# An attention and two-layer expert kernel: the upper weight words scaled on ScalarE, the first weight chunks issued by ScalarE, and four blocks of probabilities normalised in one VectorE operation

## The chip, the cores and the metric

The kernel runs on one core of a Trainium2 chip. The metric is the device time of one execution in microseconds; the median of several runs is given. One core has TensorE (matrix products, transposes), VectorE, ScalarE, GpSimd and SyncE, which in this kernel issues almost all transfers. In the profile they are called PE (its weight loads PEld), DVE, ACT, POOL and SP (its queue SPq).

## What is computed

Inputs of the two dense layers come as 64-bit floats and everything else as 32-bit floats. The reference, cut:

```python
k_all = np.concatenate([k_g, k_l], axis=2)            # 4 batches, 8 heads, 32 + 512 keys, 64 wide
out_g = softmax(scale * q_g @ k_all^T) @ v_all        # 32 global queries see everything
s_ll = where(abs(i - j) <= 32, scale * q_l @ k_l^T, -1e9)
a_l = softmax(concatenate([scale * q_l @ k_g^T, s_ll]))
out_l = a_l @ concatenate([v_g, v_l])                 # 512 local queries see a window and the global keys
x = concatenate([out_g, out_l])                       # as 2176 rows of 512
h = x @ w_in                                          # 512 x 2048
x = maximum(0.01 * h, h) @ w_out                      # 2048 x 512
expert = argmax(normalised x @ normalised emb^T / tau)
out[rows of e] = gate * (maximum(x[rows of e] @ w1[e], 0) @ w2[e])   # 8 experts, 1024 wide
```

`softmax` is the exponential of the scores less their maximum, divided by its sum plus 1e-9.

## The kernel before

The program has three stages that overlap: attention, the two dense layers, and the routed experts. TensorE's instructions stand in the order in which the program is written; the order on ScalarE, VectorE, GpSimd and SyncE is made by a scheduler, from the same program, priorities and its own table of durations. Each engine then runs its list strictly in order.

**Attention** goes by pairs of heads (16 pairs, n) and by groups of two chunks of 128 queries (32 groups, p, called S in the code). For a pair, `QK` transposes keys and queries; for a group, `S` makes eight products (L200), adds the mask and takes the maximum on VectorE (L211), takes four exponentials with their sums on ScalarE (L217), adds 1e-9 and takes the reciprocal on VectorE (L221, L222), and scales the four blocks of 224 probabilities by their reciprocals: two of the four on VectorE (L228) and two on ScalarE (L226). The blocks lie in four tiles `pr`, one for each head of two groups in turn. Later `TR` transposes the probabilities and `AV` multiplies them with the values. The work is dealt out in 68 slots, the first 21 of them alone (up to the first dense step), the rest between the steps of the dense layers.

**The weights of the dense layers** come in 32 chunks of 128 x 512, alternately from `w_in` and `w_out`, as 64-bit floats, and are made into a 32-bit float and then into a high and a low part of it. `conv_load` loads a chunk of 512 KB into one of two buffers `raw` (L343, issued by SyncE). `conv_round` reads it twice on ScalarE: L359 takes the absolute value of the upper words as 32-bit floats, L360 scales the lower words to three bits. `conv_bits` works on VectorE: a maximum with a tiny number (L368), a shift by three with a mask (L369), an operation that puts in sign and top bit from the raw upper words (L372), and the addition of the low bits (L375). `conv_split` copies the high part on ScalarE (L382) and subtracts on GpSimd (L383). One call of `conv` does split(i - 1), bits(i), round(i + 1), load(i + 2). In the first 21 slots `conv` is called in each even slot from the second on (10 times); then once a step, and more often as the dense steps ask for their chunks.

**Dense layers**: `L1` is one step of the first product (L675, 12 matmuls), the leaky ReLU with its split into two parts (L682 and L685 on ScalarE, L683 and L686 on VectorE), `L2` the second product (L697 to L699).

**The start**: keys, queries and values of the first three pairs are loaded, all by SyncE, each issue of its own (`load_qk`, `load_v`, L88 to L119), then the first two chunks of the weights.

Of the kernel before, what the change touches and what calls it, by code (L numbers as in the profile page):

```python
# [18 lines left out]
P = 128  # L19
BIG = 3.0e38  # L20
NEG = -8.0e9
TINY = 1.125 * 2.0 ** -15


@with_exitstack
def kernel(
# [55 lines left out]
    def load_qk(n):  # L82
        b, h0 = n // HP, 2 * (n % HP)
        kn = att.tile([P, NC, 2, D], F32, tag="kn", bufs=2, name="kn")
        qn = att.tile([P, NC, 2, D], F32, tag="qn", bufs=1, name="qn")
        def rows(dst, src):
            for h in range(2):
                nc.sync.dma_start(dst[:, :, h, :], src[b, h0 + h].rearrange("(c p) d -> p c d", p=P))  # L88

        rows(kn, k_l)  # L90
        if n % 2 == 0:
            gn = att.tile([2 * SG, 4 * D], F32, tag="gn", bufs=2, name="gn")
            for i, src in enumerate((k_g, q_g)):
                nc.sync.dma_start(
                    gn[i * SG:(i + 1) * SG].rearrange("s (h d) -> s h d", h=4),
                    src[b, h0:h0 + 4].rearrange("h s d -> s h d"),
                )
        else:
            gn = natural["gn"]
        rows(qn, q_l)  # L100
        natural["gn"] = gn
        natural[n] = qn, kn, gn[:, (n % 2) * 2 * D:(n % 2 + 1) * 2 * D]
# [32 lines left out]
    )  # L135
    nc.gpsimd.memset(mask[:, 0, 0:SG], NEG)
    nc.gpsimd.memset(mask[:, 2, WIN - SG:WIN], NEG)
    NPR = 4
    prs = [att.tile([P, 2, 256], F32, name=f"pr{i}") for i in range(NPR)]
    qz = att.tile([P, NC * P], F32, name="qz")  # L140
    gzs = [att.tile([P, 2, SG], F32, name=f"gz{i}") for i in range(2)]
    for t in gzs:
# [48 lines left out]
    def S(p):  # L191
# [4 lines left out]
        for i in range(2):  # L196
            c = c0 + i
            for h in range(2):
# [2 lines left out]
                    sps[h][:, i, :], qz[r, c * P:(c + 1) * P], kT[r, c, :], start=True, stop=True,  # L201
                    tile_position=(D * h, 0),
                )
        pr2 = [prs[(2 * p + h) % NPR] for h in range(2)]
        nm = att.tile([P, 4], F32, tag="nm", bufs=2, name="nm")
        sm = att.tile([P, 4], F32, tag="sm", bufs=2, name="sm")
        for h in range(2):
# [12 lines left out]
            )  # L220
        nc.vector.tensor_scalar(out=sm, in0=sm, scalar1=1e-9, scalar2=None, op0=ALU.add)  # L221
        nc.vector.reciprocal(out=sm, in_=sm)  # L222
        for j in range(4):
            pr = pr2[j // 2][:, j % 2, 0:WK]
            if j % 2:
                nc.scalar.activation(out=pr, in_=pr, func=AF.Copy, scale=sm[:, j:j + 1])  # L226
            else:
                nc.vector.tensor_scalar(out=pr, in0=pr, scalar1=sm[:, j:j + 1], scalar2=None, op0=ALU.mult)  # L228
        for h in range(2):
            units[2 * p + h] = pr2[h]  # L230

# [100 lines left out]
    def conv_load(i):  # L332
        f = i // 2
        if i % 2 == 0:
            src = w_in[:, f * P:(f + 1) * P].rearrange("(k p) f -> p k f", p=P)
            shape = [P, KM, P]
        else:
            src = w_out[f * P:(f + 1) * P, :].unsqueeze(1)
            shape = [P, 1, DM]
        if wide:  # L340
            t = att.tile([P, 2 * DM], I32, tag="raw", bufs=2, name="raw")
            t = t.rearrange("p (k n) -> p k n", k=shape[1])
            nc.sync.dma_start(t, src.bitcast(I32))  # L343
            raws[i] = t.rearrange("p k (n t) -> p k n t", t=2)
        else:
            t = att.tile([P, DM], F32, tag="raw", bufs=2, name="raw")
            t = t.rearrange("p (k n) -> p k n", k=shape[1])
            nc.sync.dma_start(t, src)
            raws[i] = t

    def conv_round(i):

        if wide and i in raws:
            pair = []
            for k in range(2):
                t = sb.tile([P, DM], I32, tag=("x2T", "x2")[k], bufs=2, name=f"t{k}")
                pair.append(t.rearrange("p (k n) -> p k n", k=raws[i].shape[1]))
            temps[i] = pair
            nc.scalar.activation(out=pair[0].bitcast(F32), in_=raws[i][:, :, :, 1].bitcast(F32), func=AF.Abs)  # L359
            nc.scalar.activation(out=pair[1], in_=raws[i][:, :, :, 0].bitcast(U32), func=AF.Copy, scale=2.0 ** -29)  # L360

    def conv_bits(i):
        if not wide or i not in raws:
            return
        raw = raws.pop(i)
        top = raw[:, :, :, 1]
        t, low = temps[i]
        nc.vector.tensor_scalar(out=t.bitcast(F32), in0=t.bitcast(F32), scalar1=TINY, scalar2=None, op0=ALU.max)  # L368
        nc.vector.tensor_scalar(  # L369
            out=t, in0=t, scalar1=3, scalar2=0x3FFFFFF8, op0=ALU.logical_shift_left, op1=ALU.bitwise_and  # L370
        )
        nc.vector.scalar_tensor_tensor(  # L372
            out=t, in0=top, scalar=-0x40000000, in1=t, op0=ALU.bitwise_and, op1=ALU.bitwise_or
        )
        nc.vector.tensor_tensor(out=t, in0=t, in1=low, op=ALU.add)  # L375
        temps[i] = t

# [562 lines left out]
        )  # L940


    QK(0, 0)
    QK(0, 1)
    for t in prs:
        nc.vector.memset(t[:, :, WK:256], 0.0)
    for ve, vb in zip(ves, vbs):
        nc.vector.memset(ve[32:64, NC], 0.0)
        nc.vector.memset(vb[96:P], 0.0)
        nc.vector.memset(vb[32:64, NC - 1], 0.0)  # L950
    load_v(0)
    load_qk(1)
    load_qk(2)
    load_v(1)
    for i in range(2):
        conv_load(i)
    conv_round(0)

    NU = 4 * NHP
# [75 lines left out]
    SLOT0 = 21  # L1035
    while slot < SLOT0:
        run(att_parts(slot))
        if slot >= 2 and slot % 2 < 1:
            conv()
        if slot == 2:  # L1040
            routing_constants()
# [7 lines left out]
    k = 0  # L1049
# [167 lines left out]
```

## Time and profile before

| | us |
|---|---|
| median of 3 runs | 940.39 (939.21 to 940.49) |
| the profiled execution | 938.37 |
| its span, first to last instruction | 936.7 |
| TensorE busy in the span | 869.3 (93%) |
| VectorE busy | 640.6 (68%) |
| ScalarE busy | 586.4 (63%) |
| GpSimd busy | 169.2 (18%) |

Busy time is the time in which an engine ran an instruction that computes. Shares of the whole span are averages over stages with different limits, so each stage has to be read for itself. The chain of work that ended last goes 69% through TensorE, 12% through VectorE, 7% through transfers. The TensorE clock is granted by the chip in two levels, and the profile shows the mean of a stretch as a share of the higher one; over the span it is 0.961.

### The profile page before, as it was taken

To read this page: it belongs to the slowest core of one execution; us is meant where nothing else is said; L and a number is where in the kernel's file an instruction comes from. 1 tells how busy PE (TensorE), PEld (TensorE's weight loads), DVE (VectorE), ACT (ScalarE), POOL (GpSimd) and SP (SyncE) were. 2 spreads that over 40 slices of the span, in tenths; PEclk is the share of its full clock that TensorE was granted. 3 is DMA by queue.
4 is the path that set the end of the run, shared out by engine and by line. 5 is a ranking of instruction groups with operands and counts; after the bars stand their busy time and mean duration, and the time that the engine had idled before them with its cause. 6 is when DMAs were issued, how large, how long until landed. Compare 5 with 4: busy or idle time off the path is not lost.

```text
span 936.7 us, 16036 instructions
## 1 busy us (share of the span) xinstructions
PE 869.3 (93%) x5578; PEld 731.6 (78%) x5578; DVE 640.6 (68%) x1623; ACT 586.4 (63%) x1270; POOL 169.2 (18%) x220
## 2 busy tenths in 40 slices
PE   6567798899999999999999999997899999999997
PEld 4445686688888888888888888985677888888885
DVE  5589889953564554463543435555989989999996
ACT  5688777754545645554533233364687888888885
POOL 2232423310100110010000000030233232231211
PEclk9777889999999999999999999997999999999999
DMA  5766455311022011110000000544315118829550
GB/s 126 196 167 156 137 145 154 109 42 29 23 65 47 20 51 39 26 39 11 1 23 1 23 1 24 180 158 112 24 57 195 53 46 300 300 62 385 199 202 26
DMA packets 104997, 92.70 MB, mean 99 GB/s; under 512 B 73735, under 2 KB 82055, under 8 KB 104914
## 3 DMA queue, kind: packets, MB, share of 16 engines
q1 hardware_dynamic: 100690, 80.87, 28.7%
q0 software_dynamic: 4224, 10.78, 4.1%
q8 instruction: 45, 0.74, 0.4%
q14 instruction: 38, 0.31, 0.1%
HBM read 140.03 MB, written 11.63 MB: 162 GB/s over the span
## 4 chain that ended last, share of the span: by engine, by line
PE 69%; DVE 12%; DMA 7%; issue 6%; ACT 4%; SPq 1%; POOL 0%; POOLq 0%; DVEq 0%; ACTq 0%
PE hps L675 19%; PE hp L901 9%; PE yp L929 8%; PE yp L697 7%; PE yp L699 6%; PE yp L698 6%; DMA raw<-in_moe_w_in_dram 3%; PE sp L200 2%; PE pp L236 2%; PE av L250 2%; DVE t L372 2%; DMA raw<-in_moe_w_out_dram 2%; PE tp L915 1%; DVE w2s L856 1%; DVE w1s L856 1%
## 5 line engine op out<-in xcount | busy, mean ns | idle before, releaser
L683 DVE SCALAR_TENSOR_TENSOR gf<-gf 128x256 f32<-128x256 f32 (+1 forms) x144 | 60.4, 427 | 125.0 <-ACT gf L682 124.8
L682 ACT COPY gf<-hps 128x256 f32<-128x256 f32 (+1 forms) x144 | 50.2, 360 | 151.5 <-PE hps L675 150.3
L901 PE MATMUL hp<-w1s,xgT 128*128 128x512 f32 x528 | 138.9, 413 | 0.0
L929 PE MATMUL yp<-w2s,ht 128*128 128x512 f32 x528 | 130.9, 396 | 1.0 <-DVEq L1181 1.0
L929 PEld LDWEIGHTS yp<-w2s,ht 128*128 128x128 f32 x528 | 98.8, 188 | 25.7 <-DVEq L1181 1.4
L901 PEld LDWEIGHTS hp<-w1s,xgT 128*128 128x128 f32 x528 | 99.8, 196 | 21.3
L697 PE MATMUL yp<-woh,g 128*128 128x512 f32 x272 | 114.9, 423 | 0.2 <-ACT g L685 0.2
L699 PE MATMUL yp<-woh,g 128*128 128x512 f32 x272 | 108.0, 397 | 1.4 <-DVE g L686 1.3
L698 PE MATMUL yp<-wol,g 128*128 128x512 f32 x272 | 107.8, 396 | 0.0
L686 DVE TENSOR_TENSOR g<-gf,g 128x256 fp32r<-128x256 f32 (+1 forms) x144 | 60.7, 430 | 38.9 <-ACT g L685 34.2
L675 PE MATMUL hps<-xs,wih 128*128 128x256 f32 x448 | 76.4, 293 | 9.5 <-ACT gf L682 6.8
L685 ACT CAST g<-gf 128x256 fp32r<-128x256 f32 (+1 forms) x144 | 55.3, 395 | 38.1 <-DVE gf L683 37.7
L675 PEld LDWEIGHTS hps<-xs,wih 128*128 128x128 f32 x448 | 65.3, 191 | 16.7 <-ACT gf L682 7.7
L675 PE MATMUL hps<-xs,wil 128*128 128x256 f32 x448 | 72.1, 283 | 0.0
L675 PE MATMUL hps<-xl,wih 128*128 128x256 f32 x448 | 72.1, 283 | 0.0
L217 ACT ACTIVATE pr<-pr,nm 128x224 f32<-128x224 f32 x128 | 60.4, 475 | 6.2 <-DVE nm L211 5.3
L699 PEld LDWEIGHTS yp<-woh,g 128*128 128x128 f32 x272 | 51.3, 189 | 15.1 <-DVE g L686 2.7
L675 PEld LDWEIGHTS hps<-xs,wil 128*128 128x128 f32 x448 | 61.8, 191 | 0.0
L675 PEld LDWEIGHTS hps<-xl,wih 128*128 128x128 f32 x448 | 61.7, 191 | 0.0
L697 PEld LDWEIGHTS yp<-woh,g 128*128 128x128 f32 x272 | 51.3, 189 | 11.9 <-issue 4.3
L856 DVE TENSOR_TENSOR w2s<-w2a,w2s 128x1024 fp32r<-128x1024 f32 x48 | 56.6, 1219 | 2.9 <-ACT w2s L855 2.9
L856 DVE TENSOR_TENSOR w1s<-w1a,w1s 128x1024 fp32r<-128x1024 f32 x48 | 56.6, 1218 | 2.0 <-ACT w1s L855 1.9
(259 smaller groups left out, 1737.3 us busy)
## 6 DMA issues: line engine op xcount, KB each, us to landing
w1a<-in_moe_w_dram SPq DMA_DIRECT2D x12, 2048.0 KB
w2a<-in_moe_w_dram SPq DMA_DIRECT2D x12, 2048.0 KB
w1b<-in_moe_w_dram SPq DMA_DIRECT2D x12, 2048.0 KB
w2b<-in_moe_w_dram SPq DMA_DIRECT2D x12, 2048.0 KB
raw<-in_moe_w_in_dram SPq DMA_DIRECT2D x16, 512.0 KB
raw<-in_moe_w_out_dram SPq DMA_DIRECT2D x16, 512.0 KB
x2d<-x SPq DMA_DIRECT2D x16, 256.5 KB
kn<-in_k_l_dram SPq DMA_DIRECT2D x32, 128.0 KB
```

Of the source, the lines that this page charges most:

```text
L217: nc.scalar.activation(out=pr, in_=pr, func=AF.Exp, bias=nm[:, j:j + 1], scale=-1.0, accum_out=sm[:, j:j + 1],)
L675: nc.tensor.matmul(hps, ws[a][:, k], xs[c][k], start=(a + c + k == 0), stop=((a, c) == (1, 0) and k == KM - 1))
L682: nc.scalar.copy(gf, hps[:, cs])
L683: nc.vector.scalar_tensor_tensor(out=gf, in0=gf, scalar=0.01, in1=gf, op0=ALU.mult, op1=ALU.max)
L685: nc.scalar.copy(g[:, 0], gf)
L686: nc.vector.tensor_tensor(out=g[:, 1], in0=gf, in1=g[:, 0].bitcast(F32), op=ALU.subtract)
L697: nc.tensor.matmul(yp, g[:, 0], hi, start=(f == 0), stop=False)
L698: nc.tensor.matmul(yp, g[:, 0], lo, start=False, stop=False)
L699: nc.tensor.matmul(yp, g[:, 1], hi, start=False, stop=(f == KF - 1))
L856: nc.vector.tensor_tensor(out=w[:, 1, c], in0=src[:, c], in1=w[:, 0, c].bitcast(F32), op=ALU.subtract)
L901: nc.tensor.matmul(hp_, xT[:, a, k, :], w[:, c, k, :], start=(a + c + k == 0), stop=(c == 1 and k == KM - 1))
L929: nc.tensor.matmul(yp, ht[:, a, f, :], w[:, c, f, :], start=(j + a + c + f == 0), stop=(j == c == 1 and f == 3))
```

## The change

Three things. First, in the conversion of the weights ScalarE scales the upper words by 2 to the power -112, which moves the exponent and lets numbers too small become zero, and keeps the sign; VectorE then needs three operations instead of four (the sign is put into the low word, the scaled word is shifted, the two are added), and none of them reads the raw chunk. Second, the loads: the second head of the first pair of heads (keys and queries) and the first six chunks of the weights are issued by ScalarE's queue instead of SyncE's, the first two chunks are called for ahead of the first attention work, the keys of the second pair ahead of the first values, and `conv` is called 14 times instead of 10 in the first 21 slots, beginning in slot 0. Third, the probabilities of a group lie in one tile of four blocks, and one VectorE operation multiplies all four by their reciprocals.

```diff
-                nc.sync.dma_start(dst[:, :, h, :], src[b, h0 + h].rearrange("(c p) d -> p c d", p=P))
+                (nc.scalar if n == 0 and h == 1 else nc.sync).dma_start(dst[:, :, h, :], src[b, h0 + h].rearrange("(c p) d -> p c d", p=P))
...
-    NPR = 4
-    prs = [att.tile([P, 2, 256], F32, name=f"pr{i}") for i in range(NPR)]
+    prs = [att.tile([P, 4, 256], F32, name=f"pr{i}") for i in range(2)]
...
-        for j in range(4):
-            pr = pr2[j // 2][:, j % 2, 0:WK]
-            if j % 2:
-                nc.scalar.activation(out=pr, in_=pr, func=AF.Copy, scale=sm[:, j:j + 1])
-            else:
-                nc.vector.tensor_scalar(out=pr, in0=pr, scalar1=sm[:, j:j + 1], scalar2=None, op0=ALU.mult)
+        nc.vector.tensor_tensor(
+            out=pr4[:, :, 0:WK], in0=pr4[:, :, 0:WK], in1=sm.unsqueeze(2).to_broadcast([P, 4, WK]), op=ALU.mult
+        )
...
-            nc.sync.dma_start(t, src.bitcast(I32))
+            (nc.scalar if i < 6 else nc.sync).dma_start(t, src.bitcast(I32))
...
-            nc.scalar.activation(out=pair[0].bitcast(F32), in_=raws[i][:, :, :, 1].bitcast(F32), func=AF.Abs)
-            nc.scalar.activation(out=pair[1], in_=raws[i][:, :, :, 0].bitcast(U32), func=AF.Copy, scale=2.0 ** -29)
+            nc.scalar.activation(out=pair[0].bitcast(F32), in_=raw[:, :, :, 1].bitcast(F32), func=AF.Copy, scale=2.0 ** -112)
+            nc.scalar.activation(out=pair[1], in_=raw[:, :, :, 0].bitcast(U32), func=AF.Copy, scale=2.0 ** -29)
...
-        nc.vector.tensor_scalar(out=t.bitcast(F32), in0=t.bitcast(F32), scalar1=TINY, scalar2=None, op0=ALU.max)
-        nc.vector.tensor_scalar(
-            out=t, in0=t, scalar1=3, scalar2=0x3FFFFFF8, op0=ALU.logical_shift_left, op1=ALU.bitwise_and
+        nc.vector.scalar_tensor_tensor(
+            out=low, in0=t, scalar=-0x80000000, in1=low, op0=ALU.bitwise_and, op1=ALU.bitwise_or
         )
-        nc.vector.scalar_tensor_tensor(
-            out=t, in0=top, scalar=-0x40000000, in1=t, op0=ALU.bitwise_and, op1=ALU.bitwise_or
-        )
+        nc.vector.tensor_scalar(out=t, in0=t, scalar1=3, scalar2=None, op0=ALU.logical_shift_left)
         nc.vector.tensor_tensor(out=t, in0=t, in1=low, op=ALU.add)
...
+    for i in range(2):
+        conv_load(i)
     QK(0, 0)
     QK(0, 1)
...
+    load_qk(1)
     load_v(0)
-    load_qk(1)
     load_qk(2)
     load_v(1)
-    for i in range(2):
-        conv_load(i)
     conv_round(0)
...
-        if slot >= 2 and slot % 2 < 1:
+        if slot % 2 < 1 or slot in (1, 3, 5):
             conv()
```

How this moves the work shows in the order of the engines' lists. ScalarE at the program's start, before (kT and qz are the copies of the first keys and queries, L217 the exponentials of the first group, L226 their scaling):

```order
L177 ACT_TABLE_LOAD
L177 COPY kT<-kp 128x4x128
L166 COPY qz<-qp 128x512
L217 ACTIVATE pr_97,sm<-pr_97,nm 128x224 x2
L217 ACTIVATE pr_98,sm<-pr_98,nm 128x224 x2
L177 COPY kT<-kp 128x4x128
L226 ACTIVATE pr_97<-pr_97,sm 128x224
L226 ACTIVATE pr_98<-pr_98,sm 128x224
```

and of the changed kernel, ScalarE from its second issue on (line numbers of the changed file: L358 and L359 are the two passes over a chunk, L340 the issue of a chunk, L165 the query copy):

```order
L88 DMA qn<-in_q_l_dram 128x4x64
L340 DMA raw<-in_moe_w_in_dram 128x4x256
L340 DMA raw<-in_moe_w_out_dram 128x1024
L176 ACT_TABLE_LOAD
L176 COPY kT<-kp 128x4x128
L358 ACTIVATE t_202<-raw 128x512
L359 ACTIVATE t_203<-raw 128x512
L340 DMA raw<-in_moe_w_in_dram 128x4x256
L358 ACTIVATE t_228<-raw 128x512
L359 ACTIVATE t_229<-raw 128x512
L340 DMA raw<-in_moe_w_out_dram 128x1024
L165 COPY qz<-qp 128x512
```

The passes over two chunks and the issue of two more now stand ahead of the first query copy and of the first exponentials.

VectorE around one group of attention and one chunk, in the middle of the first 21 slots, before (t with a number is a chunk's word tile):

```order
L369 TENSOR_SCALAR t_1171<-t_1171 128x512
L372 SCALAR_TENSOR_TENSOR t_1171<-raw,t_1171 128x512
L221 TENSOR_SCALAR sm<-sm 128x4
L375 ISA t_1171<-t_1171,t_1172 128x1024
L222 RECIPROCAL sm<-sm 128x4
L228 TENSOR_SCALAR pr_97<-pr_97,sm 128x224
L228 TENSOR_SCALAR pr_98<-pr_98,sm 128x224
```

and of the changed kernel (L365 puts the sign into the low word, L368 is the shift, L369 the addition, L223 the scaling of the group):

```order
L368 TENSOR_SCALAR t_1272<-t_1272 128x512
L369 ISA t_1272<-t_1272,t_1273 128x1024
L221 TENSOR_SCALAR sm<-sm 128x4
L222 RECIPROCAL sm<-sm 128x4
L223 TENSOR_TENSOR pr_97<-pr_97,sm 128x4x224
L365 SCALAR_TENSOR_TENSOR t_1339<-t_1338,t_1339 128x512
L368 TENSOR_SCALAR t_1338<-t_1338 128x512
```

The two scalings of a group have become one of four blocks, and no operation of a chunk reads `raw` any more. Counted over the whole of VectorE's list, 15 of the L372 and 14 of the L375 stood ahead of the first leaky ReLU (L683), with 11 groups of attention; in the changed kernel all three operations of 22 chunks stand ahead of it, and 11 groups as before. TensorE's list is the same in both.

## Rows read from the trace of the kernel before

**Rows 1.** The page, 40 equal slices of the span, tenths: TensorE, VectorE, clock.

```profile
PE   6567798899999999999999999997899999999997
...
DVE  5589889953564554463543435555989989999996
...
PEclk9777889999999999999999999997999999999999
```

**Rows 2.** Stretches: length, busy us of each engine (instructions), clock, DMA share, GB/s.

```profile
0.00:9.00 9.00, 3.56 (x15) 2.73 (x17) 3.99 (x24) 2.46 (x3) 4.28 (x27) 1.00 0.47 106
9.00:25.00 16.00, 11.88 (x91) 8.55 (x88) 9.40 (x49) 10.54 (x37) 2.23 (x8) 1.00 0.65 150
25.00:46.80 21.80, 12.87 (x106) 10.69 (x107) 12.42 (x40) 15.27 (x38) 4.97 (x6) 0.72 0.75 192
46.80:107.60 60.80, 41.25 (x321) 31.41 (x320) 54.77 (x163) 52.64 (x141) 19.26 (x23) 0.75 0.57 154
107.60:190.00 82.40, 72.94 (x521) 60.77 (x520) 75.19 (x187) 61.76 (x152) 27.67 (x27) 0.93 0.48 133
190.00:281.00 91.00, 90.96 (x729) 79.12 (x729) 47.32 (x192) 47.46 (x138) 9.08 (x15) 1.00 0.17 41
```

**Rows 3.** Groups by line, 0 to 107.6 us: xcount | busy us, mean ns | idle before.

```profile
L372 DVE SCALAR_TENSOR_TENSOR t<-raw,t 128x512 int32<-128x512 int32 x15 | 14.2, 947 | 0.3
L375 DVE CUSTOM_DVE_ANT_0 t<-t,t 128x1024 uint16<-128x1024 uint16 x14 | 11.3, 804 | 0.2
L368 DVE TENSOR_SCALAR t<-t 128x512 f32<-128x512 f32 x15 | 9.4, 628 | 10.5 <-ACT t L359 10.5
L228 DVE TENSOR_SCALAR pr<-pr,sm 128x224 f32<-128x224 f32 x22 | 7.5, 381 | 0.4
...
L226 ACT ACTIVATE pr<-pr,sm 128x224 f32<-128x224 f32 x22 | 9.5, 488 | 0.0
...
L382 ACT CAST wih<-t 128x512 fp32r<-128x512 f32 x7 | 4.4, 626 | 1.6 <-DVE t L375 1.6
```

**Rows 4.** Single lines: count, duration ns min/median/max, first and last start us.

```profile
L228 DVE TENSOR_SCALAR pr<-pr,sm x32: 323/332/1447, 12.7 to 189.1; 128x224 f32<-128x224 f32 x32
L368 DVE TENSOR_SCALAR t<-t x32: 404/422/1518, 27.5 to 186.3; 128x512 f32<-128x512 f32 x32
L369 DVE TENSOR_SCALAR t<-t x32: 404/426/1410, 27.9 to 186.8; 128x512 int32<-128x512 int32 x32
L372 DVE SCALAR_TENSOR_TENSOR t<-raw,t x32: 674/693/1777, 29.7 to 187.2; 128x512 int32<-128x512 int32 x32
L375 DVE CUSTOM_DVE_ANT_0 t<-t,t x32: 670/684/1653, 31.7 to 189.9; 128x1024 uint16<-128x1024 uint16 x32
L655 DVE TENSOR_TENSOR xl<-xr,xs x8: 410/416/449, 31.4 to 96.6; 128x256 fp32r<-128x256 f32 x8
L686 DVE TENSOR_TENSOR g<-gf,g x15: 402/418/1497, 108.9 to 185.4; 128x256 fp32r<-128x256 f32 x15
```

**Rows 5.** Waits (us, times, longest): VectorE 25 to 46.8, then SyncE's queue 0 to 200.

```profile
DVE t L368 <- ACT t L359: 8.3, 2, 5.4
...
SPq L343 <- DVE t L372: 55.0, 20, 5.3
```

**Rows 6.** Timeline of the start: start us, us, engine, line, operation, [idle before it].

```profile
7.22 0.59 ACT L166 COPY qz<-qp 128x512 f32<-128x512 f32 x1 [1.42 <-PE qp L164]
10.32 0.48 ACT L217 ACTIVATE pr<-pr,nm 128x224 f32<-128x224 f32 x1 [2.52 <-DVE nm L211]
...
22.10 0.43 SPq L343 DMA_DIRECT2D raw<-in_moe_w_in_dram  x1
...
26.79 0.66 ACT L359 ACTIVATE t<-raw 128x512 f32<-128x512 f32 x1 [3.31 <-DMA raw<-in_moe_w_in_dram]
```

**Rows 7.** Timeline around 101 us, GpSimd and VectorE.

```profile
100.70 1.46 POOL L383 TENSOR_TENSOR wil<-t,wih 128x512 fp32r<-128x512 f32 x1 [4.35 <-ACT wih L382]
...
101.08 1.64 DVE L372 SCALAR_TENSOR_TENSOR t<-raw,t 128x512 int32<-128x512 int32 x1
```

More of the change, by code (lines that the diff above doesn't have):

```diff
@@ L21 @@
 NEG = -8.0e9
-TINY = 1.125 * 2.0 ** -15
 @with_exitstack
@@ L203, in S @@
                 )
-        pr2 = [prs[(2 * p + h) % NPR] for h in range(2)]
+        pr4 = prs[p % 2]
+        pr2 = [pr4[:, 2 * h:2 * h + 2] for h in range(2)]
         nm = att.tile([P, 4], F32, tag="nm", bufs=2, name="nm")
@@ L353, in conv_round @@
         if wide and i in raws:
+            raw = raws.pop(i)
             pair = []
@@ L356, in conv_round @@
                 t = sb.tile([P, DM], I32, tag=("x2T", "x2")[k], bufs=2, name=f"t{k}")
-                pair.append(t.rearrange("p (k n) -> p k n", k=raws[i].shape[1]))
+                pair.append(t.rearrange("p (k n) -> p k n", k=raw.shape[1]))
             temps[i] = pair
-            nc.scalar.activation(out=pair[0].bitcast(F32), in_=raws[i][:, :, :, 1].bitcast(F32), func=AF.Abs)
-            nc.scalar.activation(out=pair[1], in_=raws[i][:, :, :, 0].bitcast(U32), func=AF.Copy, scale=2.0 ** -29)
+            nc.scalar.activation(out=pair[0].bitcast(F32), in_=raw[:, :, :, 1].bitcast(F32), func=AF.Copy, scale=2.0 ** -112)
+            nc.scalar.activation(out=pair[1], in_=raw[:, :, :, 0].bitcast(U32), func=AF.Copy, scale=2.0 ** -29)
     def conv_bits(i):
-        if not wide or i not in raws:
+        if i not in temps:
             return
-        raw = raws.pop(i)
-        top = raw[:, :, :, 1]
         t, low = temps[i]
-        nc.vector.tensor_scalar(out=t.bitcast(F32), in0=t.bitcast(F32), scalar1=TINY, scalar2=None, op0=ALU.max)
-        nc.vector.tensor_scalar(
-            out=t, in0=t, scalar1=3, scalar2=0x3FFFFFF8, op0=ALU.logical_shift_left, op1=ALU.bitwise_and
-        )
-        nc.vector.scalar_tensor_tensor(
-            out=t, in0=top, scalar=-0x40000000, in1=t, op0=ALU.bitwise_and, op1=ALU.bitwise_or
-        )
+        nc.vector.scalar_tensor_tensor(
+            out=low, in0=t, scalar=-0x80000000, in1=low, op0=ALU.bitwise_and, op1=ALU.bitwise_or
+        )
+        nc.vector.tensor_scalar(out=t, in0=t, scalar1=3, scalar2=None, op0=ALU.logical_shift_left)
         nc.vector.tensor_tensor(out=t, in0=t, in1=low, op=ALU.add)
```

## Prediction

> **What bounds the kernel now.** I read the slices first [rows 1]: TensorE runs at nine tenths or more almost everywhere from the ninth slice on, at full clock, while the first eight slices (about 190 us) have it at 5 to 9 tenths, five of them with the clock granted at 0.7 or 0.8. The change touches work of that stretch and hardly any other. Then the stretches [rows 2]. I set the borders at 107.6 us, the first leaky ReLU on VectorE (L683, the sign that the dense layers have begun), and at 190, the end of the weight conversion. From 46.8 to 107.6 VectorE is busy 54.77 of 60.8 us, 90%, TensorE 41.25 at a clock of 0.75. From 107.6 to 190 VectorE is busy 75.19 of 82.4 (91%), and TensorE 72.94, so it idles 9.5. From 190 to 281 TensorE has 90.96 of 91.0, VectorE only 47.32: from there nothing but TensorE counts. Up to 190 VectorE is therefore the nearest bound, and from 190 on TensorE. Before 46.8 neither is: VectorE idles 5.0 us up to 9, 6.6 up to 25 and 9.4 up to 46.8, and 8.3 of the last are one wait, the maximum L368 for ScalarE's first pass L359, which itself stood for a weight chunk [rows 5, 6].
>
> **The change, part by part.** *The conversion of a chunk* (32 of them). Before: L368 0.42, L369 0.43, L372 0.69, L375 0.68 us, medians without a collision [rows 4], 2.22 in all. After: one two-input operation (L372's price, 0.69: same size, one pass), the shift 0.43 and the same add 0.68: 1.80. It saves 0.42 us of VectorE for each chunk, 13.4 in all. ScalarE's first pass changes its function at one price, nothing gained or lost. VectorE no longer reads the raw chunk, so its buffer comes free after ScalarE's two passes; SyncE now stands 55.0 us in 20 waits for L372 before it may load the next chunk [rows 5]. That wait ends earlier and the transfers behind it in the queue too; what is late next there is the same queue's waits for TensorE, so I count nothing for it beyond a smaller idle share of VectorE, below.
>
> *The normalisation* (32 groups of two heads and two chunks; 11 before 107.6, 5 more up to 190). ScalarE loses two passes of 0.488 [rows 3], 0.97 a group. VectorE loses two of 0.33 [rows 4] and gets one of 4 x 224 = 896 columns with two inputs. No such width is in the trace. The nearest rows with two inputs are 256 columns at 0.42 (L655) and 512 at 0.69 (L372) [rows 4]: 1.05 ns a column more, so 0.69 + 384 x 1.05 ns = 1.09 us. The lower end would be no dearer than the two that go (0.66: nothing excludes a faster mode, though none shows); the upper 1.09 plus a collision, 2.04. I take 1.09, nearest to the rows: +0.43 a group, 4.7 before 107.6 and 2.2 after.
>
> *Collisions.* L372 takes 0.69, or 1.64 when it meets a GpSimd subtraction that has begun [rows 7]; means over medians in rows 3 and 4, (0.947 - 0.693) x 15 + (0.804 - 0.684) x 14 + (0.628 - 0.422) x 15 + (0.381 - 0.332) x 22, give 9.7 us over the 14 chunks done by 107.6, some 0.7 us a chunk. The change leaves the subtractions as they are, so I leave 0.7 to each chunk, on whichever operation it falls.
>
> *The order.* In the order of VectorE's queue 22 whole chunks stand ahead of the first leaky ReLU, before it 14 and the greater part of a fifteenth (14.5). The same 11 groups of attention stand ahead of it both times. So 7.5 chunks move over the border at 107.6: 7.5 x (1.80 + 0.7) = 18.8 us more ahead of it. Why this need not cost 18.8: the first of these chunks now start when VectorE has little to do. The first two loads stand at the head of ScalarE's queue instead of behind 36 issues of SyncE, where the first was issued at 22.10 and read at 26.79 [rows 6].
>
> *Sum up to the border.* VectorE was busy 3.99 + 9.40 + 12.42 + 54.77 = 80.6 [rows 2]. Now 80.6 - 15 x 0.42 + 11 x 0.43 + 18.8 = 97.8. Up to 9 us nothing changes (4.0 busy; the first chunk is not there). From 9 to 25 five chunks (9.0) and two groups ask for more than the 16 us; I take 13 busy, 3 lost. The other 80.8 run at the idle share of the steady stretch, 6.0 of 60.8 [rows 2], without its 2.2 us of standing for raw chunks: 6%. 80.8 / 0.94 = 86.0, and the border comes at 25 + 86 = **111**, 3.4 us later than before. Bounds: no idle time at all after 25 us, 105.8; a tenth idle as now and the holes before 46.8 as large as now, 122.
>
> *Sum after the border.* VectorE loses 7.5 x 2.92 and 10 x 0.42 and gets 2.2: 75.2 - 21.9 - 4.2 + 2.2 = 51.3, no longer the bound. TensorE is, with 72.9 us of work. Its clock there was 0.93 [rows 2]; at 1.00 all through the work would be 67.8. I take half of that gain, 72.9 - 2.5, and 1.5 us of idle time: 72. Bounds 69 (full clock) and 77 (four of the 9.5 idle us stay). So the state of 190 is reached at 111 + 72 = 183, **7 us earlier**. From there TensorE has the same list, 100% busy, and the stages to the end move forward whole; the dearer group (16 more, +7 us of VectorE) lies in stretches where VectorE has half its time free [rows 2].
>
> *Against its own time.* Span 936.7 becomes 929.7; with the 1.7 us around it (938.37) 931.4. The median of the runs, 940.39, is 2.0 above the profiled execution, so 933.4.
>
> *Issuing on ScalarE.* Two first attention loads and six chunks are issued there, 8 x 0.43 [rows 6] = 3.4 us, and the later four wait for a buffer and for a transfer, with the copies and exponentials behind them queued. Of the phase's ScalarE work: 7.5 x (2 x 0.66 + 0.62) [rows 6, 3] = 14.6 more, 11 x 0.97 = 10.7 less, 3.4 more, so +7.3 on its 80.9 of 107.6 [rows 2], 79% of 111: covered by VectorE as long as VectorE is fuller. What the two queues give is weighed by the rows of the transfers: the engines' share was 0.47 up to 9 us, 0.65 up to 25, 0.75 up to 46.8 [rows 2], so there is room early and little later. The Trainium skill (DMA: Bandwidth & Descriptors, "Issuing engines are not separate DMA queues") says that transfers run on the same 16 engines and interleave whoever issues them, and only issue time is saved. By that rule the early chunks take their share from the first attention loads; no row of before shows two issuers, and the sum counts no bandwidth for it.
>
> **Rivals.** *The start is held up (slower).* ScalarE's order now puts two chunks' passes ahead of the first query copy, and a third's ahead of the first exponentials; these ran at 7.22 and 10.32 [rows 6]. A chunk took 4.7 us from issue to its first pass with one other chunk in the air. Two chunks together beside the first heads would land at about 8 to 11; with four passes of 0.66 the query copy comes at 11 to 13, the exponentials at 15 to 18, 5 to 8 late. If attention and not VectorE's sum sets the border, these 8 us and about 6 of ScalarE's +7.3 pass on: 107.6 + 14 = 121.6, + 72 = 193.6, **944**. It decides from a border later than 118. For it: ScalarE is busy 52.64 of the 60.8 us up to the border [rows 2], hardly less than VectorE. Against: VectorE at 90% from 46.8 on, so that a late start is caught up. The same time comes out if the loads gain nothing and the holes before 46.8 stay as they are (border 122): the change would then not do what it says.
>
> *The wide operation collides (no change).* It has two inputs in SBUF like L686, which went from 0.42 to 1.50 in a collision [rows 4]. GpSimd is busy 31 of the 107.6 us [rows 2], so 3 of 11 groups would meet it by chance; if half do, in addition to the old collisions, 5.5 x 0.95 / 0.94 = 5.6 us: border 116.6, **939**. The Trainium skill (SBUF — State Buffer, "Who interferes with whom") says that a VectorE instruction with two SBUF inputs contends with a GpSimd instruction that reads SBUF, and that the second to start is blocked whole. By that rule every group can collide, and the wait is that of 1.64 against 0.69 [rows 7], with which the trace agrees; L655, also with two inputs, never did (0.449 at most in 8).
>
> *VectorE never idles (faster still).* Border 105.8, then 69 at full clock: 174.8, 15 earlier, **925**.
>
> **How the numbers follow.** Forecast (2 to 12 us gained): 0.47. Still faster: 0.13. Within 0.2% (1.9 us, about what a measurement of this kernel can tell from no change), mostly by collisions: 0.14. Slower, by the held start: 0.26. Faster 0.60, same 0.14, slower 0.26. The range goes from just below the fast rival to the slow one, 924 to 944; 0.2 lies outside, most of it above.
>
> **What would show it.** Right: the first leaky ReLU at 106 to 115 us, a steady TensorE from about 183, no wait of SyncE's weight loads for VectorE, L368's old wait of 8.3 us gone, the wide operation at 1.1 us, the stages after 190 unchanged in length. Wrong: a first leaky ReLU after 118; ScalarE standing for raw chunks for several us at 6 to 20 us while TensorE idles; TensorE's idle time after the border still at 9 us, which would put the bound on something other than VectorE; the wide operation at 1.5 us or more on average.

## The result and the profile after

| | before | after |
|---|---|---|
| median, us | 940.44 (939.21 to 941.12, 4 runs) | 931.25 (930.80 to 931.62, 4 runs) |
| ratio | 1 | 0.9909, 95% interval 0.9894 to 0.9925 |
| profiled execution: span, us | 936.7 | 929.1 |
| VectorE / ScalarE busy, us | 640.6 / 586.4 | 639.2 / 561.6 |

9.2 us faster; 933.4 was forecast. Of the 9.2 us 7.6 stand between the two profiled spans, for which 7 was forecast; the rest is how far each median lies from its profiled execution. The same kernel once more, on another chip and beside other runs, gave 0.9927 (0.9901 to 0.9953). The page of the kernel after, in 40 slices of the span; these lines answer to [rows 1]:

```profile
PE   3766799999999999999999999997899999999997
...
PEclk9776799999999999999999999997999999999999
```

TensorE now stands at nine tenths from the sixth slice on, instead of from the ninth. In the very first slice it fell from 6 to 3. The stretches of [rows 2] in the kernel after: length, busy us of TensorE, its weight loads, VectorE, ScalarE, GpSimd, then clock, DMA share, GB/s.

```profile
0.00:9.00 9.00, 1.43 (x5) 0.90 (x5) 3.90 (x22) 1.87 (x2) 4.28 (x27) 1.00 0.77 211
9.00:25.00 16.00, 8.53 (x41) 6.29 (x45) 12.18 (x36) 12.13 (x30) 4.38 (x5) 0.85 0.87 229
25.00:46.80 21.80, 15.38 (x146) 11.09 (x139) 19.89 (x56) 18.91 (x51) 11.57 (x13) 0.81 0.83 189
46.80:107.60 60.80, 41.89 (x334) 32.32 (x334) 55.43 (x152) 48.79 (x129) 19.49 (x23) 0.74 0.66 186
107.60:190.00 82.40, 77.14 (x618) 65.36 (x618) 59.50 (x158) 52.81 (x140) 22.83 (x23) 0.96 0.34 91
```

From 9 to 46.8 VectorE is busy 32.1 us instead of 21.8, which is the conversion brought forward; from 46.8 to 107.6 it is as full as before with ScalarE 3.9 us lighter; from 107.6 to 190 it falls from 75.2 to 59.5, and TensorE does 618 matmuls instead of 521 in the same time. From there the two kernels run alike: the 92 us from 182 to 274 hold 736 matmuls in the kernel after, the 92 us from 190 to 282 hold 733 before.

Two marks serve for all kernels below: the first and the sixteenth leaky ReLU on VectorE. First the kernel before, then the kernel after (count, duration min/median/max in ns, first and last start in us):

```profile
L683 DVE SCALAR_TENSOR_TENSOR gf<-gf x16: 409/420/1301, 107.6 to 189.4; 128x256 f32<-128x256 f32 x16
```

```profile
L677 DVE SCALAR_TENSOR_TENSOR gf<-gf x16: 395/425/1516, 109.9 to 179.2; 128x256 f32<-128x256 f32 x16
```

The first one comes 2.3 us later, the sixteenth 10.2 us earlier. By the eighteenth (188.6 against 196.3) the lead is 7.7, and with that the spans end, 7.6 apart. The sixteenth mark overstates the lead, because TensorE does not stand at the same place of its list there: by that mark it had done 1046 matmuls before (to 189.4) and 1026 after (to 179.2). Equal numbers compare better: 1047 by 190.0 us before, 1048 by 182.4 after, again 7.6 us. From its first mark to that state the kernel after takes (columns as above):

```profile
109.90:182.40 72.50, 69.43 (x528) 58.87 (x529) 54.87 (x144) 47.39 (x124) 21.92 (x23) 0.96 0.35 93
```

The groups that answer to [rows 3], 0 to 107.6 us, and the wide scaling's single durations, 0 to 190:

```profile
L365 DVE SCALAR_TENSOR_TENSOR t<-t,t 128x512 int32<-128x512 int32 x22 | 19.7, 896 | 7.7 <-ACT t L359 5.4 <-ACT t L358 2.2
L369 DVE CUSTOM_DVE_ANT_0 t<-t,t 128x1024 uint16<-128x1024 uint16 x22 | 16.8, 765 | 0.5
...
L223 DVE TENSOR_TENSOR pr<-pr,sm 128x896 f32<-128x896 f32 x10 | 12.0, 1195 | 0.2
L368 DVE TENSOR_SCALAR t<-t 128x512 int32<-128x512 int32 x22 | 11.1, 504 | 0.9
```

```profile
L223 DVE TENSOR_TENSOR pr<-pr,sm x16: 1071/1092/2170, 20.5 to 177.6; 128x896 f32<-128x896 f32 x16
```

Three operations a chunk, 22 chunks, and the wide scaling at a median of 1.092 us, which is the 1.09 worked out from rows of other widths. With the collisions its mean is 1.2 (one of the ten took 2.170). What SyncE's queue waits for, 0 to 200 us (us, times, longest), beside [rows 5]:

```profile
SPq L340 <- ACT t L358: 11.0, 7, 4.7
```

The 55.0 us of standing for VectorE are gone; the loads of weights now stand 11.0 us for ScalarE's pass L358, and the queue's longest wait is an attention load that stands for TensorE (35.9 us in six waits). The start, ScalarE's timeline, beside [rows 6]:

```profile
1.96 0.53 ACTq L340 DMA_DIRECT2D raw<-in_moe_w_in_dram  x1
...
9.02 0.66 ACT L358 ACTIVATE t<-raw 128x512 f32<-128x512 f32 x1 [3.11 <-DMA raw<-in_moe_w_in_dram]
...
12.60 0.59 ACT L165 COPY qz<-qp 128x512 f32<-128x512 f32 x1 [0.42 <-ACT t L359]
...
16.42 0.46 ACT L217 ACTIVATE pr<-pr,nm 128x224 f32<-128x224 f32 x1
```

The first query copy comes 5.4 us later than before, the first exponential 6.1 us: the hold of the slower rival took place as it was put (11 to 13, 15 to 18), and the kernel is faster all the same. One of the prediction's signs of being wrong came too: ScalarE stands 3.11 us for its first raw chunk, while TensorE stands 4.67 us up to 10.73 us for the second query load.

### The profile page after: what moved, and what is told of

Same layout as the page of the kernel before. It is cut to its first block, busy times and chain, and to the rows that moved or that the text cites. A ratio compares the mean times of both kernels' runs of the same rounds, so it can differ in the third digit from the quotient of the medians.

```text
span 929.1 us, 15882 instructions
## 1 busy us (share of the span) xinstructions
PE 863.6 (93%) x5578; PEld 727.1 (78%) x5578; DVE 639.2 (69%) x1557; ACT 561.6 (60%) x1206; POOL 173.5 (19%) x220
## 4 chain that ended last, share of the span: by engine, by line
PE 73%; DVE 9%; issue 6%; DMA 6%; ACT 5%; POOL 1%; SPq 1%; POOLq 0%; ACTq 0%; DVEq 0%
PE hps L669 20%; PE hp L895 10%; PE yp L923 9%; PE yp L691 7%; PE yp L693 6%; PE yp L692 6%; PE av L247 3%; PE pp L233 2%; PE sp L199 2%; PE tp L909 2%; DMA qn<-in_q_l_dram 1%; DMA ids<-idl 1%; ACT pr L217 1%; PE lp L499 1%; DVE pr L223 1%
## 5 line engine op out<-in xcount | busy, mean ns | idle before, releaser
L680 DVE TENSOR_TENSOR g<-gf,g 128x256 fp32r<-128x256 f32 (+1 forms) x144 | 57.7, 409 | 39.3 <-ACT g L679 35.0
L669 PE MATMUL hps<-xs,wih 128*128 128x256 f32 x448 | 75.7, 291 | 5.7 <-ACT gf L676 4.2
L217 ACT ACTIVATE pr<-pr,nm 128x224 f32<-128x224 f32 x128 | 60.6, 475 | 2.7 <-DVE nm L211 1.8
L693 PEld LDWEIGHTS yp<-woh,g 128*128 128x128 f32 x272 | 51.2, 188 | 12.7 <-DVE g L680 0.2
L691 PEld LDWEIGHTS yp<-woh,g 128*128 128x128 f32 x272 | 51.3, 189 | 11.7 <-issue 4.5
L850 DVE TENSOR_TENSOR w1s<-w1a,w1s 128x1024 fp32r<-128x1024 f32 x48 | 56.5, 1217 | 1.8 <-ACT w1s L849 1.7
```

The source lines that it names most:

```text
L217: nc.scalar.activation(out=pr, in_=pr, func=AF.Exp, bias=nm[:, j:j + 1], scale=-1.0, accum_out=sm[:, j:j + 1],)
L669: nc.tensor.matmul(hps, ws[a][:, k], xs[c][k], start=(a + c + k == 0), stop=((a, c) == (1, 0) and k == KM - 1))
L680: nc.vector.tensor_tensor(out=g[:, 1], in0=gf, in1=g[:, 0].bitcast(F32), op=ALU.subtract)
L691: nc.tensor.matmul(yp, g[:, 0], hi, start=(f == 0), stop=False)
L693: nc.tensor.matmul(yp, g[:, 1], hi, start=False, stop=(f == KF - 1))
L850: nc.vector.tensor_tensor(out=w[:, 1, c], in0=src[:, c], in1=w[:, 0, c].bitcast(F32), op=ALU.subtract)
```

## The experiments

The change has three parts: **bits** (the conversion in three operations), **early** (ScalarE's issues, early loads, 14 calls), **wide** (one scaling a group). The first theory is the prediction's: up to the first leaky ReLU the sum of VectorE's work decides, after it TensorE's; so bits gain, wide costs, early moves work into idle time. The rivals: the start carries the gain; or ScalarE is as much a bound as VectorE. The first four kernels have one part alone, or one left out.

**Bits alone.**

```diff
...
-            nc.scalar.activation(out=pair[0].bitcast(F32), in_=raws[i][:, :, :, 1].bitcast(F32), func=AF.Abs)
+            nc.scalar.activation(out=pair[0].bitcast(F32), in_=raw[:, :, :, 1].bitcast(F32), func=AF.Copy, scale=2.0 ** -112)
...
```

> The kernel before with the conversion of the change alone: scaling on ScalarE, three VectorE operations, raw chunk not read by VectorE; loads, calls and normalisation as before. VectorE theory (up to the first dense step the sum of VectorE's work decides): 15 chunks x 0.42 = 6.3 us less ahead of the border, the border at 100 to 102 instead of 107.6, of the 7 us after it little, since TensorE is nearly full there: 932 to 935 us. Start theory (the gain comes from chunks moved into idle time at the start): at most 2 us, 938 to 940.

0.9971 (0.9956 to 0.9985), 938.0 us: about 2.8 us, where 5 to 8 were expected. Its border (the first leaky ReLU) was at 110.5, not at 100 to 102: VectorE has 2.1 us less work up to it, but stands 5.4 us for a transfer, a wait that the kernel before does not have (it is looked at under "the change without wide").

**Early alone.**

```diff
...
-            nc.sync.dma_start(t, src.bitcast(I32))
+            (nc.scalar if i < 6 else nc.sync).dma_start(t, src.bitcast(I32))
...
-        if slot >= 2 and slot % 2 < 1:
+        if slot % 2 < 1 or slot in (1, 3, 5):
```

> The kernel before with the loads and calls of the change alone: two first loads and six chunks issued by ScalarE, early loads, 14 calls; four operations a chunk, normalisation as before. VectorE theory: 19 instead of 14.5 chunks ahead of the border, 4.5 x 2.9 = 13 us more there against about 12 us of idle time filled, border 1 to 3 us later; 13 us of VectorE less after it, where TensorE idles 9.5: 935 to 938. Start theory: this part carries the gain, 931 to 934.

0.9986 (0.9971 to 1.0001), 939.5 us: the start theory (931 to 934) falls, at least for this part by itself, and the VectorE theory (935 to 938) is missed as well.

**Wide alone.**

```diff
...
-            if j % 2:
-                nc.scalar.activation(out=pr, in_=pr, func=AF.Copy, scale=sm[:, j:j + 1])
-            else:
-                nc.vector.tensor_scalar(out=pr, in0=pr, scalar1=sm[:, j:j + 1], scalar2=None, op0=ALU.mult)
+        nc.vector.tensor_tensor(
+            out=pr4[:, :, 0:WK], in0=pr4[:, :, 0:WK], in1=sm.unsqueeze(2).to_broadcast([P, 4, WK]), op=ALU.mult
+        )
```

> The kernel before with the wide normalisation alone. VectorE theory: 11 x 0.43 = 4.7 us more ahead of the border and some collisions, 5 to 7 us later, 943 to 947. ScalarE theory (ScalarE, 87% busy up to the border, is as much the bound; two passes of 0.49 a group leave it): no change or a gain, 936 to 941.

0.9970 (0.9955 to 0.9985), 938.7 us. The VectorE theory forecast 943 to 947 here and is wrong; the ScalarE theory has it, and the waits point the same way: VectorE stood 10.5 us for ScalarE's pass over the chunks up to the border before [rows 3], and 4.9 here (against that 3.4 us of standing for a transfer came in, see the next experiment).

**The change without wide** (that diff the other way round, in the changed kernel).

> The changed kernel with the old normalisation (two scalings on VectorE, two on ScalarE). VectorE theory: 4.7 us less ahead of the border, 926 to 928. ScalarE theory: 15 us more on ScalarE up to 190, equal or slower, 931 to 936.

0.9961 (0.9934 to 0.9987), 937.0 us, some 4 to 6 slower than the change: again the opposite of the VectorE theory, and 1 us above the ScalarE theory's range. The stretch from 46.8 to each kernel's border, first without wide, then the kernel after (same columns as above):

```profile
46.80:114.90 68.10, 42.87 (x343) 32.35 (x342) 56.48 (x167) 58.42 (x153) 22.27 (x25) 0.75 0.63 172
```

```profile
46.80:109.80 63.00, 41.91 (x335) 32.34 (x335) 57.54 (x156) 50.99 (x136) 20.31 (x24) 0.74 0.64 182
```

Without wide ScalarE is the fuller of the two, 58.4 against 56.5 us of 68.1; with it VectorE does 1.1 us more, ScalarE 7.4 less, and the stretch is 5.1 us shorter. Neither is full. Over the whole way to the border VectorE has 4.4 us less work without wide and stands 9.5 us longer, 25.8 against 16.3. Of the 9.5, some 2.5 are waits for ScalarE and 2.9 for TensorE; 4.2 are a single wait, first without wide, then the kernel after (us, times, longest):

```profile
DVE xl L651 <- DMA x2d<-blank: 4.8, 1, 4.8
```

```profile
DVE xl L649 <- DMA x2d<-blank: 0.6, 1, 0.6
```

It stands ahead of the split of the second block of x (at 48.1 and 48.6 us). In the code the tile `xl` shares four buffers with a tile of zeros, from which SyncE issues four transfers (one into `idl`, three into `x2d`), and the operation waits for four semaphores; so these transfers are the likely cause, though the profile, which infers the name, does not always name them. No part of the change aims at this wait, and no run here tests it; so ScalarE's time is only a part of what leaving wide out cost.

To price the two engines apart I put idle work on one of them.

**ScalarE loaded**, and **VectorE loaded**, each with three operations a group that read a constant and write a tile nobody reads:

```diff
+        for _ in range(3):
+            nc.scalar.activation(out=dmy, in_=ident[:, 0:100], func=AF.Copy, scale=0.5)
```

```diff
+        for _ in range(3):
+            nc.vector.tensor_scalar(out=dmy, in0=ident[:, 0:100], scalar1=0.5, scalar2=None, op0=ALU.mult)
```

The changed kernel again, as their neighbour:

> The changed kernel once more, beside the next three on one chip: 930 to 933 us, by every theory.

933.1 us (930.8 to 937.0), 0.9927.

> The changed kernel with three passes of 100 columns more on ScalarE in each attention group, from a constant into a tile nobody reads: about the 0.97 us a group that the change takes off ScalarE. They do nothing for the result. ScalarE theory (what the wide normalisation gains is ScalarE's time): 4 to 6 us slower than the changed kernel, 935 to 937. Chain theory (what it gains is that a group's probabilities no longer wait for two engines): within 1.5 us of it. VectorE theory: no change.

1.0001 (0.9981 to 1.0020), 940.4 us.

> The changed kernel with three operations of 100 columns more on VectorE in each group, from a constant into a tile nobody reads: some 0.7 us a group, 7 us up to the first dense step. They do nothing for the result. VectorE theory: 6 to 9 us slower than the changed kernel, 937 to 940. If ScalarE were the only bound: within 1.5 us of it. If both are bounds in turn: 2 to 5 us slower.

1.0080 (1.0050 to 1.0110), 947.0 us. Both are dearer than expected, and the rows say why in part. First ScalarE's group of added passes up to 119.8 us, its border, then VectorE's up to 126.3:

```profile
L228 ACT ACTIVATE dmy<-ident 128x100 f32<-128x100 f32 x63 | 17.8, 282 | 0.9 <-ACT dmy L228 0.5
```

```profile
L228 DVE TENSOR_SCALAR dmy<-ident 128x100 f32<-128x100 f32 x96 | 28.9, 301 | 1.0
```

Since the added work waits for nothing, the scheduler put it earlier than the groups it was written for: 63 of ScalarE's 96 passes and all 96 of VectorE's (spread from 3.4 to 98.6 us) stand ahead of the border, where 33 were meant. So the runs are prices, at other amounts than planned: 17.8 us of ScalarE put the border 7 to 10 us later (119.8 against 112.5 and 109.9), 28.9 of VectorE 14 to 16 us (126.3). But these sums count the overlap of one instruction with the next. Counted as time in which the engine is busy at all, up to the border, VectorE rose by 16.7 us (93.6 to 110.3, with one chunk fewer) and ScalarE by 12.7 (84.0 to 96.7, with VectorE at 95.4). So a microsecond in which VectorE is really occupied went with 0.8 to 1.0 us of border here, one of ScalarE with 0.6 to 0.8. The chain theory (no cost from work that nobody waits for) falls too.

So these are not clean prices of the two engines. With ScalarE loaded VectorE did not stand longer for ScalarE after the first 9 us (8.4 us against 8.9 in the change); it stood 5.5 us instead of 0.6 for the transfer ahead of the split of x, and 4.0 instead of 0.4 for TensorE. Whether the added passes made those late or the new order of the lists did, these runs do not show. With VectorE loaded the same wait was 4.1 us.

**Four scalings instead of the wide one**, in the changed kernel:

```diff
-        nc.vector.tensor_tensor(
-            out=pr4[:, :, 0:WK], in0=pr4[:, :, 0:WK], in1=sm.unsqueeze(2).to_broadcast([P, 4, WK]), op=ALU.mult
-        )
+        for j in range(4):
+            pr = pr2[j // 2][:, j % 2, 0:WK]
+            nc.vector.tensor_scalar(out=pr, in0=pr, scalar1=sm[:, j:j + 1], scalar2=None, op0=ALU.mult)
```

> The changed kernel with the four blocks of a group scaled by four VectorE operations of 0.33 us instead of one wide one of 1.09: ScalarE as free as in the change, VectorE 0.23 us a group more. ScalarE theory and chain theory: 931 to 934. If the single wide operation itself were what helps (fewer instructions, fewer collisions): 935 to 938, like the changed kernel without it.

0.9994 (0.9976 to 1.0012), 939.8 us: nothing of the gain is left, and both ranges are exceeded. Its group of scalings, 0 to 118.7 us (xcount | busy, mean ns | idle before):

```profile
L225 DVE TENSOR_SCALAR pr<-pr,sm 128x224 f32<-128x224 f32 x44 | 21.1, 536 | 0.2
```

Alone such an operation takes 0.33 us [rows 4]; here the mean is 0.536: ten of the 44 took 0.88 to 1.40 us, all ten beside an operation of GpSimd, the others at most 0.36. Four short operations offer four chances of such a meeting. Four cost 2.14 us a group, the wide one 1.19; without collisions it would be 1.33 against 1.09, so the wide one is the shorter either way, and collisions widen the distance. I had seen the collision as the wide operation's risk; in VectorE's time it is its advantage. What that is worth in the kernel's time is not shown: VectorE's work up to the border is 93.9 us, as in the change, since two chunks fewer stand ahead of it, and the border still comes 6 to 9 us later, with 3.6 us of the wait for the transfer in it.

**All loads issued by SyncE again**, in the changed kernel:

```diff
...
-            (nc.scalar if i < 6 else nc.sync).dma_start(t, src.bitcast(I32))
+            nc.sync.dma_start(t, src.bitcast(I32))
```

> The changed kernel with all loads issued by SyncE again; early calls, 14 calls, conversion and normalisation as in the change. By the order 17 instead of 22 chunks stand ahead of the first dense step and no chunk ahead of the first query copy. Start theory (chunks in idle time at the start): the early start is lost, 935 to 938. Hold theory (what ScalarE's queue does at the start costs more than it brings): equal or faster than the changed kernel, 928 to 932.

0.9972 (0.9949 to 0.9995), 939.2 us, with runs from 931.7 to 941.0: the hold theory is not borne out by the median, and the spread leaves the size open.

**Without the small addition**, a trial at a better version:

```diff
-        nc.vector.tensor_scalar(out=sm, in0=sm, scalar1=1e-9, scalar2=None, op0=ALU.add)
```

> The changed kernel without the addition of 1e-9 to the sums of the window softmax, L221 of VectorE. Each sum holds the exponential of zero for the row's maximum, so it is at least 1 and the addition changes no bit of a 32-bit float. 0.18 to 0.25 us of VectorE less a group, 11 groups ahead of the border: 2.5 us of VectorE, one hop less between the exponentials and the scaling. Both engines as bounds: 1 to 3 us faster than the changed kernel, 929 to 932. If other waits decide: no change, 931 to 934.

0.9979 (0.9961 to 0.9996), 937.4 us. Less work, and some 4 to 6 us slower than the change. Nothing but 32 short operations was taken out, yet the list that the scheduler makes differs: 21 chunks stand ahead of the border instead of 22, and VectorE, with 3.0 us less work up to the border, stands 4.8 us longer ahead of the split of x, where nothing was edited:

```profile
DVE xl L648 <- DMA ve<-in_v_l_dram: 5.4, 1, 5.4
```

The border came at 112.6, and from it to the sixteenth leaky ReLU it took 73.0 us instead of 69.3. That stretch, first in this kernel, then in the kernel after:

```profile
112.60:185.60 73.00, 68.78 (x505) 57.07 (x505) 54.99 (x138) 47.42 (x123) 20.90 (x23) 0.93 0.37 100
```

```profile
109.90:179.20 69.30, 66.23 (x506) 55.96 (x507) 53.74 (x141) 45.99 (x121) 21.92 (x23) 0.96 0.36 98
```

505 and 506 matmuls, 68.78 and 66.23 us: 2.6 of the 3.7 us are the same matmuls at a lower mean clock, 0.93 against 0.96, the rest idle time. So an edit that only takes a little work away makes this kernel slower by half a percent.

**The change without bits, and without early.** The diffs of the first two experiments the other way round.

> The changed kernel with the old conversion (four VectorE operations a chunk, raw chunk read by VectorE). 20 chunks ahead of the border, each 0.42 us dearer: 8.4 us of VectorE. VectorE as a bound at the 0.57 us of border a us that the run with added VectorE work showed: 4 to 5 us slower than the changed kernel, 936 to 938. If the parts only add up as they did alone (bits 2.8, early 1.3, wide 2.0): 936 to 937 too; if bits need nothing else, 934 to 935.

1.0045 (1.0028 to 1.0061), 944.0 us: slower than the kernel before, and well beyond every expectation. (The 0.57 in the text is the 16.4 us of border for the 28.9 us of added durations.)

> The changed kernel with the old loads and calls (all by SyncE, chunks after the first three pairs, 10 calls from slot 2 on); new conversion and wide normalisation. 17 chunks ahead of the border. If the parts add up as alone: 936. Start theory (most of the gain is conversion moved into idle time at the start): 937 to 940. If the freed VectorE and ScalarE time is the gain and the start hardly counts: 932 to 934.

0.9937 (0.9916 to 0.9957), 933.5 us: as expected if the start hardly counts, and the change's time, without its whole part on the loads and calls. Its marks are 103.7 and 177.9 us. The border comes 6 to 9 us earlier than in the change, the stretch behind it is 4.9 us longer: the five chunks more that early puts ahead of the border cost there at least what they save behind it. (The profiled execution took 929.8 us, the fastest of the six, so its marks may lie some us early.)

All kernels together. V and S are VectorE's and ScalarE's busy us up to the border; chunks are those that stand whole ahead of it in VectorE's list; transfer is VectorE's wait for a transfer ahead of a split of x. All but median and ratio come from one execution of each kernel, and executions of one kernel lie up to 9 us apart:

| kernel | median | ratio | chunks | V | S | border | 16th | between | transfer |
|---|---|---|---|---|---|---|---|---|---|
| before | 940.4 | 1 | 14 | 80.6 | 80.9 | 107.6 | 189.4 | 81.8 | 0 |
| bits | 938.0 | 0.9971 | 15 | 78.5 | 81.6 | 110.5 | 186.2 | 75.7 | 5.4 |
| early | 939.5 | 0.9986 | 19 | 88.7 | 86.0 | 109.6 | 188.5 | 78.9 | 5.1 |
| wide | 938.7 | 0.9970 | 15 | 82.8 | 73.3 | 106.2 | 186.3 | 80.1 | 3.4 |
| bits, early | 937.0 | 0.9961 | 22 | 89.2 | 91.8 | 115.0 | 184.2 | 69.2 | 4.8 |
| bits, wide | 933.5 | 0.9937 | 17 | 81.2 | 75.6 | 103.7 | 177.9 | 74.2 | 3.3 |
| early, wide | 944.0 | 1.0045 | 20 | 99.7 | 81.3 | 116.2 | 192.1 | 75.9 | 0 |
| all: the change | 931.3 | 0.9909 | 22 | 93.6 | 84.0 | 109.9 | 179.2 | 69.3 | 0.6 |
| the change again | 933.1 | 0.9927 | 22 | 93.9 | 83.9 | 112.5 | 181.8 | 69.3 | 1.7 |
| ScalarE loaded | 940.4 | 1.0001 | 22 | 95.4 | 96.7 | 119.8 | 188.8 | 69.0 | 5.5 |
| VectorE loaded | 947.0 | 1.0080 | 21 | 110.3 | 84.6 | 126.3 | 195.3 | 69.0 | 4.1 |
| four scalings | 939.8 | 0.9994 | 20 | 93.9 | 82.2 | 118.7 | 188.4 | 69.7 | 3.6 |
| SyncE issues | 939.2 | 0.9972 | 17 | 80.8 | 76.8 | 108.3 | 185.0 | 76.7 | 0.8 |
| no small addition | 937.4 | 0.9979 | 21 | 90.6 | 82.9 | 112.6 | 185.6 | 73.0 | 5.4 |

Three things can be read from it. The column "between" goes with the chunks left over: 69 to 70 us where at least 20 chunks were done (but 73.0 and 75.9 in two), 74 to 77 at 15 to 17 with the new conversion, 79 to 82 with the old one. (In the kernel before and in wide alone TensorE is some 20 matmuls further at the sixteenth mark than in the others, so their 81.8 and 80.1 are too long by 2 to 3 us against the rest.) At 69 TensorE is nearly full, 66.23 of 69.3 us in the change. Second, the border goes with VectorE's work: a plane through the 14 points, fitted by least squares, is 44 + 0.51 V + 0.27 S, with a scatter of 2.6 us about it. With VectorE alone it is 59 + 0.59 V and a scatter of 3.0, so the fit hardly tells ScalarE's share. Third, the change has a short wait for the transfer, 0.6 and 1.7 us, and of the five kernels made from it that lie at 937 to 940.4 four wait 3.6 to 5.5. But without bits there is no wait at 944.0, and SyncE issues has 0.8 at 939.2, so this wait is not the whole of it either. How much of a part's price it is stays open.

## Why the prediction was right, point by point

The forecast of 7 us was near. Its second half, behind the border, came out in mechanism and in size. In the first half several steps were off and largely cancelled, so that the border came where it was put is in part luck.

- **After the border** (forecast 72 us, bounds 69 and 77): 72.5 to the same state of TensorE, which the kernel before reaches at 190 and the kernel after at 182.4 (forecast 183). TensorE became the bound as put, at a clock of 0.96, the half of the gain that was taken; it was busy 69.4 us where 70.4 were taken and idle 3.1 where 1.5 were. VectorE's 51.3 us was near (54.87 of 72.5). Of the eight kernels with at least 20 chunks ahead of the border six agree; without bits and without the small addition the stretch is longer.
- **The border** (forecast 111, bounds 105.8 and 122): 109.9 and 112.5. The sum of VectorE's work was to be 97.8 and was 93.6 up to 109.9. Collisions were dearer in my sum, 0.7 us a chunk: the means over the medians, (0.896 - 0.692) x 22 + (0.765 - 0.691) x 22 + (0.504 - 0.426) x 22, give 0.36 a chunk, and 0.1 a group for the wide operation. The sum also added durations of single operations to busy time, which leaves out their overlap. Against that VectorE idled 16.3 us, where the sum left 13.2 (111 less 97.8); the 2.2 us taken out of the idle share were waits for ScalarE's pass, and after 46.8 us VectorE still stands 3.7 for it. Work 4.2 us too much and idle time 3.1 too little: that is the luck.
- **A microsecond of VectorE counted in full** ("run at the idle share of the steady stretch"): not borne out in general. Loaded, VectorE cost 14 to 16 us of border for 28.9 us by durations, as the prediction sums them, or for 16.7 by busy time; the plane fitted through the table gives 0.51 for busy time; and bits alone, which takes 6.3 us of durations away, gave 2.8 where 5 to 8 were expected. The wait for the transfer differs among these runs by up to 5 us, so they don't settle which price holds for an edit like these.
- **ScalarE "covered by VectorE as long as VectorE is fuller"**: not borne out. Up to the border of the kernel before ScalarE was as full as VectorE, 80.9 and 80.6 us [rows 2], and for the change alone VectorE is the fuller (93.6 and 84.0). In the loaded run 12.7 us more of ScalarE went with a border 7 to 10 us later, though VectorE had 9.6 us more work to cover it with; how much of that is ScalarE's own stays open, as said there. Wide alone shows ScalarE's part best: its passes were waited for 5.6 us less, and the border came 1.4 us earlier in spite of VectorE's added work. I had the row against my step in the rival, 52.64 of 60.8 us [rows 2], and used it only for the held start.
- **The normalisation**: price right (1.09 us, measured 1.092), sign of its effect wrong. Forecast as 4.7 us lost ahead of the border; alone and within the change it gains, 2 to 6 us. ScalarE loses 10.7 us of work and the group meets GpSimd once instead of up to twice. How much of the gain is which stays open: by the fitted plane its 4.4 us more of V and 7.8 less of S would about cancel, and within the change 4.2 us go with the shorter wait for the transfer.
- **Early as the use of idle time**: chunks did move (22 as counted) and VectorE's idle time before 46.8 went from 21.0 to 10.8 us, as forecast. The 8.3 us ahead of L368 between 25 and 46.8, which were two waits and not one, became 1.5. But it gave nothing that can be measured: 0.9937 without it, 0.9909 and 0.9927 with it, the intervals overlap. Up to the border VectorE has 12 us more work with it and 4 to 6 us less idle time. That the hold at the start takes a share is not shown: with SyncE issuing all loads the kernel was slower, not faster.
- **The rivals**: the hold at the start was real and was caught up, since VectorE filled the time with conversion. The collisions of the wide operation occur (2.170 at most) but raise its mean by 0.1 us. The Trainium skill (SBUF — State Buffer, "Who interferes with whom") allows them for a VectorE instruction with two SBUF inputs beside a GpSimd instruction that reads SBUF; the same section of the Trainium skill counts a scaling by one value among those that can contend. The trace agrees, with 0.536 us on average for the four scalings, the dearer form here.

Bits is the part without which the rest loses: early and wide both put work on VectorE (V 99.7, the highest of the unloaded kernels) and bits takes 0.42 us a chunk off it. Alone the three give 0.29, 0.14 and 0.30%, 0.73% together, and the whole 0.73 to 0.91%; but early and wide without bits lose 0.45%, so they do not simply add. Since leaving out 32 small additions costs half a percent, a difference of 4 us between two of these kernels is no proof of the work in it, and that holds for the prices of the single parts above. The order of the lists is then the likelier cause, with the wait ahead of the split of x as the one place where the traces show it; I cannot set it apart further with these runs. No kernel tried beats the change.

## What to carry to other kernels

Where two engines hand work to each other and both are busy for three quarters of a stretch or more, do not sum one of them as the bound; load each, and then read which waits grew, since the added work may not be what was waited for. One wide operation can be cheaper than several short ones that another engine blocks from time to time. Where a scheduler makes the lists, run an edit of no weight beside the real ones, to know how much the order alone can move, and look for single long waits that come and go with it. Compare two kernels where the bounding engine has done the same work, not at a mark on another engine.

## What was not expected of the hardware

A scaling of 128 x 224 by one value per row takes 0.33 us undisturbed and 0.536 on average with GpSimd at work, while the multiplication of 128 x 896 with two inputs takes 1.09 and 1.19: the long operation loses a tenth, the short one six tenths. And of ScalarE's first two transfers of 512 KB, issued at 1.96 and 2.52 us beside the first heads, the first was read 7.1 us after issue (9.02) and the second 8.4 (10.94), where the first chunk of the kernel before took 4.7 [rows 6]; the DMA share of the first 9 us rose from 0.47 to 0.77, and TensorE stood 4.67 us for the second query load.
